# Random-feature attention with two gated layers on one core: the feature projections of units 4 to 15 as pairs of half-height float32 products

## The chip, the cores and the metric

The kernel runs on one core of one Trainium2 chip. The metric is the device time of one execution in microseconds (us), as the median of three executions. Everything below is read from one profiled execution of the kernel before the change. The engines are TensorE (PE, with its weight loads listed apart as PEld), VectorE (DVE), ScalarE (ACT), GpSimd (POOL), and SyncE (SP), which only issues transfers here.

## The reference

Three stages follow one another. The first is attention with random features for 4 batches of 8 heads, 576 rows of 64 numbers and 128 features; the other two are a gated layer over 2304 tokens and a softly routed layer of 8 experts.

```python
def phi(x):
    proj = np.einsum('bhsd,md->bhsm', x, omega)
    sq = np.sum(x * x, axis=-1, keepdims=True) / 2.0
    h = proj - sq
    h = h - np.max(h, axis=-1, keepdims=True)
    return np.exp(h) / np.sqrt(m)
q_p, k_p = (phi(q_s), phi(k_s))
kv = np.einsum('bhsm,bhsd->bhmd', k_p, v)
z = np.sum(k_p, axis=2)
num = np.einsum('bhsm,bhmd->bhsd', q_p, kv)
den = np.einsum('bhsm,bhm->bhs', q_p, z)[..., None] + 1e-06
...
x = _moe_ref(x=x, **moe_kwargs)      # sigmoid(x @ w_gate) * (x @ w_val) @ w_out
return _moe2_ref(x=x, **moe2_kwargs) # soft routing into 8 experts of 4 slots
```

The change touches only `proj`, and how the features `h` are kept and turned.

## The kernel before, in words

A **unit** is one batch and two heads; there are 16, four for each batch. The two heads of a unit share the 128 partitions of a tile: head 0 has its 64 numbers on partitions 0 to 63, head 1 on 64 to 127. The 576 rows of K and of Q come as four whole tiles of 128 rows each; the last 64 rows of K and the last 64 of Q share one more tile, the tail. So a unit has nine tiles to project.

For each unit these pieces of code run:

- `load_unit` and `prep_qk` fetch the rows and compute their squared norms into `SQ`. From unit 10 on (`N_PROJ`), `prep_qk` also splits K and Q into a high and a low part (`hi_of` with the engines of `SITE["hqk"]`, `lo_of` with `SITE["lqk"]`), in a second format (fp32r).
- `chunk_proj(u, i)` makes the features in five chunks: K tiles 0 and 1, K tiles 2 and 3, the tail, Q tiles 0 and 1, Q tiles 2 and 3. A tile is one product of TensorE: the tile stands still in the array, and `obf`, 128 rows by 256 columns, streams past it. `obf` holds the feature matrix twice, for head 0 in rows 0 to 63 and columns 0 to 127, for head 1 in the other rows and columns, with zeros elsewhere. Units 0 to 9 do this in float32; units 10 to 15 use `three`, which is three products of the split parts. Each chunk fills one bank of PSUM. VectorE then takes each 128 by 128 piece out of it, adds the norm and finds the row's extreme (`tensor_tensor_reduce`), and ScalarE takes the exponential of each piece.
- `chunk_kv` multiplies the K features with V: 10 products of 128 columns, in float32.
- `chunk_qT` turns the Q features with TensorE. For the tail it turns only the lower 64 partitions of the tile: two transposes of 64 partitions.
- `chunk_num` makes numerator and denominator, half the rows at a time. For units 0 to 9 these are float32 products of 288 columns that write to 64 partitions each.

K features, Q features and tail features have one buffer each (`HK`, `HQ`, `HT`), so the features of unit u+1 can be written only when unit u has read its own.

The gated layer (`gate`, `val`, `down`) is by far the most work: per step 36 fp32r products, mostly of 512 columns, into the PSUM banks `ga`, `va` and `o0` to `o3`. It runs through `GROUPS` of token blocks. Block j needs the attention of batch j.

The order of the work is not the order of the code. `Plan.schedule` records all instructions, gives each a cost (`Plan.cost`) and a key (its due time less a lead), and lists them engine by engine. Each engine then works strictly in the order that it was given. The attention and the routed layer share two PSUM banks named `fl` (`NFL` = 2); at the start they may also use `o0` to `o3`. A tile of `fl` that is used for the first time needs a free bank, and in the plan it is parked until there is one. Some element-wise work may go to either of two engines, as `SITE` lists them.

Of the kernel before, what the change touches and what calls it, by code (L numbers as in the profile page):

```python
# [45 lines left out]
SITE = {  # L46
    "hqk": ("DVE", "ACT"), "lqk": ("POOL", "DVE"), "hqt": ("ACT", "DVE"),
    "hx": ("ACT", "DVE"), "lx": ("POOL", "DVE"), "hg": ("DVE", "ACT"),
# [7 lines left out]
T0 = -60  # L56
N_PROJ = 10
N_NUM = 10
# [26 lines left out]
SIZE = {F32: 4, F32R: 4, I32: 4, U32: 4, I64: 8}  # L85
HOP = 0.16


# [10 lines left out]
class Plan:  # L99


    def __init__(self, nc):
        self.eng = {"PE": nc.tensor, "ACT": nc.scalar, "DVE": nc.vector, "POOL": nc.gpsimd, "SP": nc.sync}
        self.ops = []
        self.tiles = {}
        self.tags = {}
        self.t = 0.0
        self.lead = {}
        self.floor = 0.0
        self.floors = []  # L110
        self.hist = {}


# [22 lines left out]
    def add(self, alts):  # L136
# [4 lines left out]
        if "out" not in kw and rest:  # L141
            outs.append(rest.pop(0))
        ins += rest
        i = len(self.ops)
        pe = alts[0][0] == "PE"
# [33 lines left out]
    def cost(self, eng, method, kw, outs, ins):  # L179


        o = outs[0] if outs else None
# [30 lines left out]
    def schedule(self):  # L213
# [12 lines left out]
        nv = n  # L226
        dyn_of = [None] * n
        left = {}
        for tag, info in self.tags.items():
            gens = info["gens"]  # L230
            if info["dyn"]:
                for g, acc in enumerate(gens):
                    left[tag, g] = len(acc)
                    for a in acc:
                        dyn_of[a] = (tag, g)
                continue
# [85 lines left out]
        while ev:  # L322
            now = ev[0][0]
            while ev and ev[0][0] <= now + 1e-9:
                _, kind, x = heapq.heappop(ev)
                if kind == 1:
                    offer(x)
                elif kind == 2:
                    d = dyn_of[x]
                    left[d] -= 1  # L330
                    if left[d] == 0:
                        room[d[0]] += 1
                        for p in parked[d[0]]:
                            offer(p)
                        parked[d[0]] = []
            for e in E:
                while free_at[e] <= now + 1e-9:
# [4 lines left out]
                    backlog[p[0]] -= self.cost(p[0], p[1], p[3], ops[i][4], ops[i][5])[0]  # L342
                    d = dyn_of[i]
                    if d and d not in live:
                        if room[d[0]] == 0:
                            if i not in parked[d[0]]:
                                parked[d[0]].append(i)
                            continue
                        room[d[0]] -= 1
                        live.add(d)  # L350
                    alts, _, _, _, outs, ins, lazy = ops[i]
# [18 lines left out]
                    heapq.heappush(ev, (free_at[e], 0, -1))  # L370
                    if d:
                        heapq.heappush(ev, (end + HOP, 2, i))
# [4 lines left out]
    def issue(self):  # L377
        for _, _, (e, method, a, k) in self.schedule():
            getattr(self.eng[e], method)(*a, **k)  # L379


def body(ctx, tc, nc, qkT, tok, von, omT, wall, phi, w1, w2, ident_d, srep_d, rrep_d, mask_d, out):
# [70 lines left out]

    q0, q1 = region(0, F32), half_region(0, F32)
# [3 lines left out]
    QT = KV = XK = XQ = obh = obl = None  # L458

    def split_regions():  # L460

        nonlocal QT, KV, XK, XQ, obh, obl
        g0, g1 = region(0, F32R), half_region(1, F32R)
        QT = carve(g0, 0, [2, 2, S])
        KV = carve(g0, 2304, [2, 2, 128])
        XK = carve(g0, 2816, [2, 640])
        XQ = carve(g1, 0, [2, 512])
        obh = carve(g1, 1024, [256])
        obl = carve(g1, 1280, [256])
        hi_of(obh, obf, ("DVE",))  # L470
        lo_of(obl, obf, obh, ("DVE",))

# [4 lines left out]
    obf = carve(g3, 3712, [256])  # L477
    HK = carve(g4, 0, [4, 2, M])
    HQ = carve(g4, 1024, [4, 2, M])
    HT = carve(g4, 2048, [1, 2, M])  # L480
    RR = [carve(g4, 2304 + 288 * k, [HALF]) for k in range(2)]
# [3 lines left out]
    SQ = carve(g4, 3712, [18])  # L485
    MX = [carve(g4, 3730 + 8 * k, [2, 4]) for k in range(6)]
    ring = {}
# [21 lines left out]
    def prep_qk(u, kind):  # L509

        if u >= NU:
            return
        if u == N_PROJ and kind == 0:
            split_regions()
        x, c, t, n = ((XK, slice(0, 640), 0, 5), (XQ, slice(640, 1152), 5, 4))[kind]
        src = QKTs[u % 2][:, c]
# [10 lines left out]
    def prep_first(a, e):  # L527
# [4 lines left out]
        DVE.tensor_reduce(out=SQ[:, 2 * a:2 * e], in_=w, axis=AX.X, op=ALU.add)  # L532

    def chunk_proj(u, i):
# [6 lines left out]
        psv = ps.rearrange("p (t m) -> p t m", t=2)  # L541
        for t in range(nt):
            c = slice(c0 + 128 * t, c0 + 128 * t + 128)
# [4 lines left out]
        n = 2 * nt  # L548
        sq = SQ[:, g0:g0 + n]
        flat = ps.rearrange("p (g m) -> p g m", m=M)[:, 0:n, :]  # L550
        hv = hb.rearrange("p t h m -> p (t h) m")
        low = turn(MX, "mx")[:, 0, 0:n]
        for g in range(n):
            DVE.tensor_tensor_reduce(out=hv[:, g], in0=flat[:, g], in1=sq[:, g:g + 1].to_broadcast([128, M]),
                                     scale=1.0 / 16.0, scalar=BIG, op0=ALU.add, op1=ALU.min, accum_out=low[:, g:g + 1])
        for g in range(n):
            ACT.activation(out=hv[:, g], in_=hv[:, g], func=AF.Exp, scale=-1.0, bias=low[:, g:g + 1])

    def chunk_kv(u):

        ps = bank()[:, 0:256].rearrange("p (h c) -> p h c", h=2)
        for h in range(2):
            for t in range(NT):
                k = HK[:, t, h, :] if t < 4 else HT[:, 0, h, :]
                PE.matmul(ps[:, h, :], k, Vs[u % 2][:, t, h, :], start=t == 0, stop=t == NT - 1)
# [7 lines left out]
    def chunk_qT(u, i):  # L573
        ps = bank().rearrange("p (h n) -> p h n", h=2)
        n = (256, 256, 64)[i]
        for h in range(2):
            if i == 2:
                PE.transpose(ps[:, h, 0:64], HT[64:128, 0, h, :], ident[64:128, 64:128])
                continue
            for t in range(2):  # L580
                PE.transpose(ps[:, h, 128 * t:128 * t + 128], HQ[:, 2 * i + t, h, :], ident)
        if u < N_NUM:
            copy(QTF[:, :, 256 * i:256 * i + n], ps[:, :, 0:n], SITE["hqt"])
            return
        qh, ql = (QT[:, l, :, 256 * i:256 * i + n] for l in range(2))
        hi_of(qh, ps[:, :, 0:n], SITE["hqt"])
        lo_of(ql, ps[:, :, 0:n], qh, ("DVE",))

# [37 lines left out]
    def step_chunks(u):  # L626
# [11 lines left out]
        def last():  # L638
            chunk_proj(v, 4)
            prep_qk(u + 2, 0)  # L640

        c = [kv, P(0), lambda: chunk_qT(u, 0), P(1), lambda: chunk_qT(u, 1), lambda: chunk_qT(u, 2), P(2),
             lambda: chunk_num(u, 0), P(3), lambda: chunk_num(u, 1), last]
        own = (0, 2, 4, 5, 7, 9)
        if v >= NU:
# [442 lines left out]
    prep_first(0, 2)  # L1088
    chunk_proj(0, 0)
    prep_first(2, 5)  # L1090
    prep_qk(0, 1)
    chunk_proj(0, 1)
    chunk_proj(0, 2)
    SP.dma_start(out=TOK, in_=tok[1])
    SP.dma_start(out=Vs[1], in_=von[1])
    chunk_proj(0, 3)
    chunk_proj(0, 4)
    prep_qk(1, 0)
# [185 lines left out]
```

## Time and profile before

| | |
|---|---|
| median of 3 runs | 703.87 us (703.55 to 704.65) |
| span of the profiled execution, first to last instruction | 702.4 us |
| TensorE busy | 678.3 us, 97% |
| VectorE, ScalarE busy | 445.7 and 443.1 us, 63% each |
| GpSimd busy | 301.3 us, 43% |

The page gives no other time for the profiled execution than its span. The span is 1.5 us (0.2%) under the median of the runs; the times of rows below are added up against the span, and the difference is then taken from the median. Rows of a timeline give the start, the length from the first start to the last end, the engine, and the operation with its count. A float32 product stands in the trace as two rows (the order of the program has 2 where the trace has 4), an fp32r product or a transpose as one.

### The profile page before, as it was taken

What the parts mean: (1) busy time and instruction counts of PE and PEld (TensorE: products, weight loads), DVE (VectorE), ACT (ScalarE), POOL (GpSimd) and SP (SyncE); (2) the same over time, 40 slices, a digit from 0 to 9 for tenths busy, and PEclk for the clock granted to TensorE, in tenths of its full rate; (3) what the DMA queues carried; (4) which work ended last, traced back from release to release, by engine and by line L of the source; (5) the groups of instructions that cost most, each with busy time, mean ns of one, the idle gap of its engine ahead of it and who ended that gap; (6) DMA issues with size and microseconds to landing.
All of it is one profiled execution on the core that took longest, in us unless ns stands there. A gap on an engine that the chain in (4) does not pass through costs nothing.

```text
span 702.4 us, 12029 instructions
## 1 busy us (share of the span) xinstructions
PE 678.3 (97%) x4095; PEld 543.9 (77%) x4095; DVE 445.7 (63%) x1292; ACT 443.1 (63%) x987; POOL 301.3 (43%) x255
## 2 busy tenths in 40 slices
PE   8999999999989999999999999999999999999993
PEld 6677667777767788788888888778888788998662
DVE  4898997899997554657476765555454335766221
ACT  5999898888777565856567674654444444765021
POOL 0356545546454444644444444354444444642000
PEclk9999999999999999999999999999999999999998
DMA  7878777677866335443333334469422228557897
GB/s 279 297 253 308 249 229 255 227 257 271 267 238 201 123 114 206 148 133 108 133 135 132 90 115 142 127 231 330 166 91 90 91 83 281 168 162 250 320 407 235
DMA packets 50124, 139.47 MB, mean 199 GB/s; under 512 B 5520, under 2 KB 11152, under 8 KB 50064
## 3 DMA queue, kind: packets, MB, share of 16 engines
q1 hardware_dynamic: 45456, 121.94, 51.9%
q10 hardware_dynamic: 4608, 16.78, 6.9%
q8 instruction: 32, 0.52, 0.3%
q14 instruction: 28, 0.23, 0.1%
HBM read 124.54 MB, written 14.16 MB: 197 GB/s over the span
## 4 chain that ended last, share of the span: by engine, by line
PE 67%; DVE 4%; issue 3%; ACT 2%; DMA 2%; POOL 1%; POOLq 0%; ACTq 0%; DVEq 0%
PE o L379 19%; PE ga L379 18%; PE va L379 18%; PE fl L379 12%; DVE x2T L379 2%; DMA ws<-wscr 1%; DVE g L379 1%; DVE ga_a L379 1%; ACT ga_a L379 1%; DMA g<-in_wall 1%; POOL w L379 1%; ACT g L379 0%; ACT XT L379 0%; ACT gt L379 0%; ACT x2T L379 0%
## 5 line engine op out<-in xcount | busy, mean ns | idle before, releaser
L379 POOL TENSOR_TENSOR w<-ws,w 128x512 fp32r<-128x512 f32 x141 | 188.3, 1336 | 235.7 <-ACT w L379 132.5
L379 PE MATMUL ga<-XT,w 128*128 128x512 f32 (+1 forms) x720 | 169.4, 377 | 1.8 <-DVE ga_a L379 1.0
L379 PE MATMUL va<-XT,w 128*128 128x512 f32 (+1 forms) x720 | 167.6, 376 | 1.2 <-DVE ga_a L379 1.2
L379 PE MATMUL o<-gt,w 128*128 128x512 f32 (+1 forms) x720 | 165.3, 374 | 0.9 <-ACT w L379 0.8
L379 PEld LDWEIGHTS ga<-XT,w 128*128 128x128 f32 x720 | 123.8, 189 | 28.1 <-issue 3.0
L379 PEld LDWEIGHTS va<-XT,w 128*128 128x128 f32 x720 | 123.5, 189 | 27.1 <-issue 3.7
L379 PEld LDWEIGHTS o<-gt,w 128*128 128x128 f32 x720 | 123.6, 189 | 25.1 <-issue 2.6
L379 ACT ACTIVATE g<-g 128x128 f32<-128x128 f32 (+3 forms) x340 | 121.1, 415 | 18.9 <-DVE g L379 12.9
L379 ACT ACTIVATE w<-ws 128x512 fp32r<-128x512 f32 x107 | 67.3, 629 | 61.9 <-issue 19.8
L379 PE MATMUL fl<-g,g 128*128 128x128 f32 (+2 forms) x514 | 87.8, 343 | 3.2 <-DVE g L379 2.1
L379 PEld LDWEIGHTS fl<-g,g 128*128 128x128 f32 (+1 forms) x514 | 61.8, 179 | 22.5 <-issue 6.6
L379 ACT ACTIVATE ga_a<-ga_a 128x512 f32<-128x512 f32 (+1 forms) x120 | 70.2, 585 | 12.6 <-DVE ga_a L379 11.5
L379 ACT ACTIVATE ga_a<-ga 128x512 f32<-128x512 f32 (+1 forms) x60 | 33.2, 554 | 65.4 <-PE ga L379 65.3
L379 DVE CUSTOM_DVE_ANT_0 g<-fl,g 128x128 f32<-128x128 f32 x242 | 56.9, 286 | 19.5 <-PE fl L379 19.0
L379 DVE SCALAR_TENSOR_TENSOR ga_a<-ga,ga_a 128x512 f32<-128x512 f32 (+1 forms) x60 | 38.2, 636 | 46.4 <-ACT ga_a L379 46.1
L379 DVE CAST w<-ws 128x512 fp32r<-128x512 f32 x55 | 23.8, 432 | 67.8 <-PE ga L379 38.1
L379 ACT ACTIVATE x2T<-g 128x512 f32<-128x512 f32 x72 | 45.9, 670 | 5.8 <-DVE x L379 5.7
L379 DVE TENSOR_SCALAR x2T<-x2T 128x512 f32<-128x512 f32 (+1 forms) x72 | 47.7, 670 | 0.9 <-ACT x2T L379 0.8
L379 DVE TENSOR_TENSOR ga_a<-va,ga_a 128x512 f32<-128x512 f32 (+1 forms) x60 | 38.0, 634 | 15.3 <-ACT ga_a L379 11.9
L379 POOL TENSOR_TENSOR XT<-g,XT 128x288 fp32r<-128x288 f32 (+2 forms) x46 | 31.3, 690 | 32.0 <-ACT XT L379 29.5
L379 ACT ACTIVATE ga_a<-ga_a,one_b 128x512 f32<-128x512 f32 (+1 forms) x60 | 40.8, 679 | 1.2
L379 DVE TENSOR_TENSOR g<-fl,g 64x288 f32<-64x288 f32 (+3 forms) x57 | 27.6, 485 | 15.5 <-ACT g L379 12.5
(200 smaller groups left out, 752.6 us busy)
## 6 DMA issues: line engine op xcount, KB each, us to landing
ws<-wscr SPq DMA_DIRECT2D x42, 512.0 KB, 3.6
ws<-wscr SPq DMA_DIRECT2D x78, 256.0 KB, 2.8
g<-in_wall SPq DMA_DIRECT2D x36, 512.0 KB, 4.9
g<-in_von SPq DMA_DIRECT2D x16, 640.0 KB, 5.1
wscr<-x SPq DMA_DIRECT2D x36, 256.0 KB, 4.5
g<-in_qkT SPq DMA_DIRECT2D x15, 576.0 KB, 4.8
g<-in_tok SPq DMA_DIRECT2D x15, 576.0 KB, 5.0
g<-in_w ACTq DMA_DIRECT2D x16, 512.0 KB, 5.2
```

Source lines behind the costliest of these rows:

```text
L379: getattr(self.eng[e], method)(*a, **k)
```

## The change

Units 4 to 15 project a group of four tiles (K, and again Q) in one go. Each tile is now two products, one for each head: head h uses only the 64 partitions of its half, for the tile as well as for the feature matrix, so that 128 columns stream instead of 256. The products of head 0 write to one bank, those of head 1 to a second. The eight products are recorded as one item (`together`) that the plan places in one piece, with its two banks. The tail remains one product of 256 columns. Units 0 to 3 keep their five chunks (`ROWS` = 4). All units now project in float32, so the split of K and Q from unit 10 on is gone, with its buffers. In place of them there are two buffers each for K, Q and tail features, by turns of units. `chunk_qT` turns the whole tail tile (128 partitions) and copies the half that it needs. In `Plan.cost` three numbers change, and `schedule` can handle an item with two banks.

```diff
 def chunk_proj(u, i):
-        x, c0, nt, hb, g0 = ((XK, 0, 2, HK[:, 0:2], 0), (XK, 256, 2, HK[:, 2:4], 4), (XK, 512, 1, HT, 8),
-                             (XQ, 0, 2, HQ[:, 0:2], 10), (XQ, 256, 2, HQ[:, 2:4], 14))[i]
-        ps = bank()
...
-            if u < N_PROJ:
-                PE.matmul(psv[:, t], QKTs[u % 2][:, 640 * (i > 2) + c0 + 128 * t:][:, 0:128], obf, start=True, stop=True)
-            else:
-                three(psv[:, t], (x[:, 0, c], x[:, 1, c]), (obh, obl))
...
+        c0, nt, hb, t0, g0 = PARTS[i]
+        hb = hb[u % 2][:, t0:t0 + nt]
+        x = QKTs[u % 2][:, c0:c0 + 128 * nt]
...
+            ps = [bank()[:, 0:128 * nt].rearrange("p (t m) -> p t m", m=M) for _ in range(2)]
...
+                if nt < 4:
+                    PE.matmul(both[:, t].rearrange("p h m -> p (h m)"), x[:, 128 * t:128 * t + 128], obf,
+                              start=True, stop=True)
+                    continue
+                for h in range(2):
+                    r = slice(64 * h, 64 * h + 64)
+                    PE.matmul(ps[h][:, t], x[r, 128 * t:128 * t + 128], obf[r, 128 * h:128 * h + 128],
+                              start=True, stop=True)
+        plan.together(products, [SQ[:, g0:g0 + 2 * nt]], [hb])
...
+        for h in range(2):
+            for t in range(nt):
+                g = 2 * t + h
+                DVE.tensor_tensor_reduce(out=hb[:, t, h], in0=ps[h][:, t],
 def prep_qk(u, kind):
-        if u >= N_PROJ:
-            hi_of(x[:, 0, :], src, SITE["hqk"])
-            lo_of(x[:, 1, :], src, x[:, 0, :], SITE["lqk"])
 def chunk_qT(u, i):
-                PE.transpose(ps[:, h, 0:64], HT[64:128, 0, h, :], ident[64:128, 64:128])
+                PE.transpose(ps[:, h, 0:128], HTs[u % 2][:, 0, h, :], ident)
 def step_chunks(u):
+        if v < ROWS:
+            c = [kv, P("K0"), qT[0], P("K1"), qT[1], qT[2], P("T"), num[0], P("Q0"), num[1], last]
+        else:
+            c = [kv, P("K"), qT[0], qT[1], qT[2], P("T"), num[0], num[1], last]
 def cost(self, eng, method, kw, outs, ins):
-                return max(n / 600.0, 0.21) / 2 + 0.02, False
-            return (0.416 if ins[0].ap[0][1] == 64 else max(0.222, n / 600.0)), False
+                return max(n / 600.0, 0.21) / 2 + 0.12, False
+            return (max(0.222, n / 600.0) / 2 if ins[0].ap[0][1] == 64 else max(0.222, n / 600.0)), False
...
-                return 0.16 + ni / 960.0, False
+                return 0.075 + ni / 960.0, False
```

How this moves the work on TensorE is seen in two places of its order. In the rows, `ga`, `va` and `o0` to `o3` are products of the gated layer; `fl` are the two shared banks, with the number of the tile. `g2` holds K and Q, `g3` the feature matrix and V, `g4` and `g1b` the features.

The first place is unit 6, in the first group of the gated layer. Before, TensorE has there the product of K features and V (10 products), the two K chunks of unit 7, the transposes of Q between them, and the tail's transposes of 64 columns:

```order
L379 MATMUL fl_197<-g3_78,g4_79 128x128 x10
L379 MATMUL fl_198<-g3_78,g2_77 128x256 x2
L379 MATMUL fl_202<-ident_63,g4_79 128x128 x4
L379 MATMUL ga_216<-XT_96,w0_201 128x512 x5
L379 MATMUL fl_203<-g3_78,g2_77 128x256 x2
L379 MATMUL fl_207<-ident_63,g4_79 128x128 x4
L379 MATMUL va_222<-XT_96,w1_206 128x512 x4
L379 MATMUL fl_208<-ident_63,g4_79 128x64 x2
```

Of the change, at the same place:

```order
L402 MATMUL fl_198<-g3_79,g4_80 128x128 x10
L402 MATMUL va_206<-XT_97,w1_190 128x512 x10
...
L402 MATMUL fl_202<-g3_79,g2_78 128x128
L402 MATMUL fl_203<-g3_79,g2_78 128x128
L402 MATMUL fl_202<-g3_79,g2_78 128x128
L402 MATMUL fl_203<-g3_79,g2_78 128x128
...
L402 MATMUL ga_216<-XT_97,w0_201 128x512 x6
L402 MATMUL fl_204<-ident_63,g4_80 128x128 x4
L402 MATMUL ga_216<-XT_97,w0_201 128x512 x2
L402 MATMUL fl_205<-ident_63,g4_80 128x128 x4
L402 MATMUL ga_216<-XT_97,w0_201 128x512
L402 MATMUL fl_209<-ident_63,g4_80 128x128 x2
```

Where two chunks of two products of 256 columns stood apart, eight products of 128 columns now stand in one piece (four of them are shown) and go by turns to two banks. The tail's transposes are 128 columns wide.

The second place is the step from unit 10 to unit 11, where the projection was in three fp32r products for each tile. Before:

```order
L379 MATMUL fl<-g_78,g_79 128x128 x10
L379 MATMUL o_257<-gt,w_343 128x512 x3
...
L379 MATMUL fl<-g1b,g_311 128x256 x6
L379 MATMUL ga<-XT,w_348 128x512 x12
L379 MATMUL fl<-ident,g_79 128x128 x4
L379 MATMUL va<-XT,w_352 128x512 x12
L379 MATMUL fl<-g1b,g_311 128x256 x6
```

Of the change:

```order
L402 MATMUL fl<-g_79,g_80 128x128 x10
L402 MATMUL o_258<-gt,w_342 128x512 x3
...
L402 MATMUL fl<-g_79,g_78 128x128 x8
L402 MATMUL ga<-XT,w_347 128x512 x12
L402 MATMUL fl<-ident,g_80 128x128 x4
L402 MATMUL va<-XT,w_352 128x512 x12
L402 MATMUL fl<-ident,g_80 128x128 x4
```

Twelve products of 256 columns in two chunks have become eight products of 128 columns in one, and the gated layer's products around them stay whole.

## Rows read from the trace of the kernel before

**Rows 1.** The page: busy times, and 40 slices (tenths).

```profile
PE 678.3 (97%) x4095; PEld 543.9 (77%) x4095; DVE 445.7 (63%) x1292; ACT 443.1 (63%) x987; POOL 301.3 (43%) x255
...
PEclk9999999999999999999999999999999999999998
```

**Rows 2.** Windows: start, end, length, busy time (count) of PE, PEld, DVE, ACT, POOL, clock.

```profile
0.00:31.00 31.00, 27.81 (x141) 20.30 (x141) 17.89 (x95) 21.70 (x60) 6.00 (x11) 1.00 0.83 294
31.00:143.00 112.00, 110.48 (x585) 81.05 (x584) 98.77 (x359) 101.42 (x262) 59.10 (x54) 1.00 0.76 253
143.00:275.00 132.00, 127.89 (x627) 101.35 (x626) 101.61 (x242) 95.56 (x200) 62.96 (x50) 1.00 0.62 206
275.00:345.00 70.00, 69.40 (x401) 57.52 (x400) 42.52 (x129) 46.43 (x99) 36.57 (x32) 1.00 0.42 140
345.00:478.00 133.00, 132.43 (x725) 110.38 (x725) 80.91 (x240) 82.54 (x178) 58.31 (x50) 1.00 0.44 145
```

**Rows 3.** Waits of PE: who waited for whom, us, times, longest.

```profile
PE fl L379 <- DVE g L379: 5.2, 9, 1.8
```

**Rows 4.** Timeline of PE: the gated layer's products alone, then 10 float32 products of 128 columns.

```profile
152.93 0.62 PE L379 MATMUL o<-gt,w 128*128 128x512 f32 x2
153.38 0.61 PE L379 MATMUL ga<-XT,w 128*128 128x512 f32 x2
153.84 0.62 PE L379 MATMUL va<-XT,w 128*128 128x512 f32 x2
154.29 1.98 PE L379 MATMUL o<-gt,w 128*128 128x512 f32 x8
156.10 2.39 PE L379 MATMUL fl<-g,g 128*128 128x128 f32 x20
158.25 0.94 PE L379 MATMUL ga<-XT,w 128*128 128x512 f32 x3
```

**Rows 5.** Timeline of PE around a float32 chunk of two tiles (unit 8).

```profile
149.19 1.20 PE L379 MATMUL va<-XT,w 128*128 128x512 f32 x4
150.22 1.02 PE L379 MATMUL fl<-g,g 128*128 128x256 f32 x4
150.89 1.28 PE L379 MATMUL va<-XT,w 128*128 128x512 f32 x4
```

**Rows 6.** Timeline of PE around an fp32r chunk of two tiles (unit 10).

```profile
230.97 0.85 PE L379 MATMUL o<-gt,w 128*128 128x512 f32 x3
231.66 0.88 PE L379 MATMUL fl<-g1b,g 128*128 128x256 f32 x6
232.37 1.09 PE L379 MATMUL ga<-XT,w 128*128 128x512 f32 x4
```

**Rows 7.** Timeline of PE around one and around two pairs of 64-column-half products.

```profile
103.22 1.29 PE L379 MATMUL o<-gt,w 128*128 128x512 f32 x5
104.45 0.71 PE L379 MATMUL fl<-g,g 128*64 128x288 f32 x4
105.08 0.96 PE L379 MATMUL o<-gt,w 128*128 128x512 f32 x3
...
243.70 1.07 PE L379 MATMUL ga<-XT,w 128*128 128x512 f32 x4
244.70 1.19 PE L379 MATMUL fl<-g,g 128*64 128x288 f32 x8
245.82 1.43 PE L379 MATMUL va<-XT,w 128*128 128x512 f32 x5
```

**Rows 8.** Timeline of PE around the tail's transposes, and around four whole transposes.

```profile
92.39 0.85 PE L379 MATMUL o<-gt,w 128*128 128x512 f32 x3
93.17 0.34 PE L379 MATMUL fl<-ident,g 64*128 64x64 f32 x2
93.44 0.73 PE L379 MATMUL o<-gt,w 128*128 128x512 f32 x2
...
193.97 1.31 PE L379 MATMUL o<-gt,w 128*128 128x512 f32 x5
195.12 0.60 PE L379 MATMUL fl<-ident,g 128*128 128x128 f32 x4
195.47 0.93 PE L379 MATMUL ga<-XT,w 128*128 128x512 f32 x3
```

**Rows 9.** Groups of PE between 31 and 143 us: count, busy us, mean ns, idle before.

```profile
L379 PE MATMUL fl<-g,g 128*128 128x256 f32 x90 | 23.8, 386 | 0.7 <-DVE g L379 0.7
...
L379 PE MATMUL o<-g,g 128*128 128x256 f32 x18 | 4.8, 391 | 0.0
...
L379 PE MATMUL fl<-ident,g 64*128 64x64 f32 x10 | 1.7, 247 | 0.0
...
L379 PE MATMUL o<-ident,g 64*128 64x64 f32 x2 | 0.3, 248 | 0.0
```

**Rows 10.** Groups over the whole span: the splits of K in units 10 to 15.

```profile
L379 POOL TENSOR_TENSOR g<-g,g 128x640 fp32r<-128x640 f32 x5 | 8.0, 1606 | 2.9 <-ACT g L379 2.4 <-issue 0.5
...
L379 DVE CAST g<-g 128x640 fp32r<-128x640 f32 x4 | 3.0, 747 | 1.1 <-PE fl L379 1.1
```

**Rows 11.** Timeline of DVE in a chunk of unit 5: the extremes of four pieces.

```profile
67.81 0.28 DVE L379 CUSTOM_DVE_ANT_0 g<-fl,g 128x128 f32<-128x128 f32 x1
...
68.43 0.09 DVE L379 DVE_READ_ACCUMULATOR2_ANT g<- 128x1 f32 x1
```

More of the change, by code (lines that the diff above doesn't have):

```diff
@@ L56 @@
 T0 = -60
-N_PROJ = 10
+N_SPLIT = 10
 N_NUM = 10
@@ L86 @@
 HOP = 0.16
+TURN = 0.2
+ROWS = 4
 class Eng:
@@ L111, in __init__, with together @@
         self.hist = {}
+        self.bundle = None
+    def together(self, calls, first=(), then=()):
+        self.bundle = []
+        calls()
+        parts, self.bundle = self.bundle, None
+        self.place([(parts[0][0][0], "together", (), {"parts": parts})],
+                   [o for _, outs, _ in parts for o in outs] + list(then),
+                   [i for _, _, ins in parts for i in ins] + list(first))
     def tile(self, pool, shape, dtype, tag, bufs=1, dyn=False):
@@ L143, in add, with place @@
         ins += rest
+        if self.bundle is not None:
+            self.bundle.append((alts[0], outs, ins))
+        else:
+            self.place(alts, outs, ins)
+    def place(self, alts, outs, ins):
         i = len(self.ops)
@@ L179, in cost @@
     def cost(self, eng, method, kw, outs, ins):
+        if method == "together":
+            return TURN * (len(kw["parts"]) > 2) + sum(self.cost(eng, a[1], a[3], o, i)[0] for a, o, i in kw["parts"]), False
         o = outs[0] if outs else None
@@ L226, in schedule @@
         nv = n
-        dyn_of = [None] * n
+        dyn_of = [[] for _ in range(n)]
         left = {}
@@ L328, in schedule @@
                 elif kind == 2:
[L329 to L335, printed above, removed]
+                    for d in dyn_of[x]:
+                        left[d] -= 1
+                        if left[d] == 0:
+                            room[d[0]] += 1
+                            for p in parked[d[0]]:
+                                offer(p)
+                            parked[d[0]] = []
             for e in E:
@@ L342, in schedule @@
                     backlog[p[0]] -= self.cost(p[0], p[1], p[3], ops[i][4], ops[i][5])[0]
[L343 to L347, printed above, removed]
+                    fresh = [d for d in dyn_of[i] if d not in live]
+                    if fresh:
+                        tag = fresh[0][0]
+                        first = any(ops[q][1] < ops[i][1] for q in parked[tag])
+                        if room[tag] < len(fresh) or first:
+                            if i not in parked[tag]:
+                                parked[tag].append(i)
                             continue
-                        room[d[0]] -= 1
-                        live.add(d)
+                        room[tag] -= len(fresh)
+                        live.update(fresh)
                     alts, _, _, _, outs, ins, lazy = ops[i]
@@ L378, in issue @@
         for _, _, (e, method, a, k) in self.schedule():
-            getattr(self.eng[e], method)(*a, **k)
+            for e, method, a, k in [p[0] for p in k["parts"]] if method == "together" else [(e, method, a, k)]:
+                getattr(self.eng[e], method)(*a, **k)
 def body(ctx, tc, nc, qkT, tok, von, omT, wall, phi, w1, w2, ident_d, srep_d, rrep_d, mask_d, out):
@@ L477, in body @@
     obf = carve(g3, 3712, [256])
-    HK = carve(g4, 0, [4, 2, M])
-    HQ = carve(g4, 1024, [4, 2, M])
-    HT = carve(g4, 2048, [1, 2, M])
+    HKs = [carve(r, 0, [4, 2, M]) for r in (g4, q2)]
+    HQs = [carve(r, 1024, [4, 2, M]) for r in (g4, q2)]
+    HTs = [carve(g4, at, [1, 2, M]) for at in (2048, 3792)]
     RR = [carve(g4, 2304 + 288 * k, [HALF]) for k in range(2)]
@@ L485, in body @@
     SQ = carve(g4, 3712, [18])
-    MX = [carve(g4, 3730 + 8 * k, [2, 4]) for k in range(6)]
+    MX = [carve(g4, 3730 + 8 * k, [8]) for k in range(6)]
     ring = {}
@@ L548, in chunk_proj @@
[L548 to L557, printed above, removed]
+        c0, nt, hb, t0, g0 = PARTS[i]
@@ new lines, in chunk_proj, with products @@
+        hb = hb[u % 2][:, t0:t0 + nt]
+        x = QKTs[u % 2][:, c0:c0 + 128 * nt]
+        if nt < 4:
+            both = bank()[:, 0:256 * nt].rearrange("p (t h m) -> p t h m", h=2, m=M)
+            ps = [both[:, :, h] for h in range(2)]
+        else:
+            ps = [bank()[:, 0:128 * nt].rearrange("p (t m) -> p t m", m=M) for _ in range(2)]
+        def products():
+            for t in range(nt):
+                if nt < 4:
+                    PE.matmul(both[:, t].rearrange("p h m -> p (h m)"), x[:, 128 * t:128 * t + 128], obf,
[5 more added lines that the diff above has]
+                              start=True, stop=True)
@@ new lines, in chunk_proj @@
+        plan.together(products, [SQ[:, g0:g0 + 2 * nt]], [hb])
+        low = turn(MX, "mx")
+        for h in range(2):
+            for t in range(nt):
+                g = 2 * t + h
+                DVE.tensor_tensor_reduce(out=hb[:, t, h], in0=ps[h][:, t],
+                                         in1=SQ[:, g0 + g:g0 + g + 1].to_broadcast([128, M]),
+                                         scale=1.0 / 16.0, scalar=BIG, op0=ALU.add, op1=ALU.min,
+                                         accum_out=low[:, g:g + 1])
@@ L559, in chunk_kv @@
+        for h in range(2):
+            for t in range(nt):
+                g = 2 * t + h
+                ACT.activation(out=hb[:, t, h], in_=hb[:, t, h], func=AF.Exp, scale=-1.0, bias=low[:, g:g + 1])
     def chunk_kv(u):
@@ L563, in chunk_kv @@
             for t in range(NT):
-                k = HK[:, t, h, :] if t < 4 else HT[:, 0, h, :]
+                k = HKs[u % 2][:, t, h, :] if t < 4 else HTs[u % 2][:, 0, h, :]
                 PE.matmul(ps[:, h, :], k, Vs[u % 2][:, t, h, :], start=t == 0, stop=t == NT - 1)
@@ L638, in last @@
         def last():
-            chunk_proj(v, 4)
+            chunk_proj(v, "Q1" if v < ROWS else "Q")
             prep_qk(u + 2, 0)
-        c = [kv, P(0), lambda: chunk_qT(u, 0), P(1), lambda: chunk_qT(u, 1), lambda: chunk_qT(u, 2), P(2),
-             lambda: chunk_num(u, 0), P(3), lambda: chunk_num(u, 1), last]
-        own = (0, 2, 4, 5, 7, 9)
+        qT = [lambda i=i: chunk_qT(u, i) for i in range(3)]
+        num = [lambda i=i: chunk_num(u, i) for i in range(2)]
+        if v < ROWS:
+            c = [kv, P("K0"), qT[0], P("K1"), qT[1], qT[2], P("T"), num[0], P("Q0"), num[1], last]
+            own = (0, 2, 4, 5, 7, 9)
+        else:
+            c = [kv, P("K"), qT[0], qT[1], qT[2], P("T"), num[0], num[1], last]
+            own = (0, 2, 3, 4, 6, 7)
         if v >= NU:
```

50 lines of the change are left out of this document (21 added, 29 removed).

## The prediction, made before the changed kernel ran

> **What bounds the kernel now.** I read the page first. TensorE is busy for 97% of the span, no other engine for more than 63%, and its granted clock is full in all slices but the last [rows 1]. So time taken from TensorE's own work is time saved, where TensorE does not wait for somebody else. The windows tell where that is [rows 2]. From 275 to 478 us TensorE is busy for 99.4% and VectorE and ScalarE for 61 and 64%: whatever TensorE is spared there comes off the span. From 31 to 143 us TensorE is busy for 110.5 of 112.0 us, but ScalarE for 101.4 and VectorE for 98.8; both together have 200.2 of 224 us filled. TensorE leads there by little. Before 31 us it is idle for 3.2 us, and the units that run there keep most of their old form. Of its own waits, the one for VectorE to empty an `fl` bank is the largest, and it is 5.2 us in 9 times [rows 3].
>
> A busy time of TensorE does not tell what a group costs, since products overlap in it. I use ends instead. The gated layer's products of 512 columns follow one another at (154.29 - 152.93)/6 = 0.227 us [rows 4]. Where a group stands between two rows of such products, its cost is the end of the row behind less the end of the row ahead, less 0.227 us for each product of the row behind. So:
>
> - float32 chunk of two tiles: (150.89 + 1.28) - (149.19 + 1.20) - 4 x 0.227 = 0.87 us, or 0.436 a tile [rows 5].
> - fp32r chunk of two tiles: 233.46 - 231.82 - 0.91 = 0.73 us, or 0.366 a tile [rows 6].
> - 10 float32 products of 128 columns: 159.19 - 156.27 - 0.68 = 2.24 us, and each is two rows, so 0.112 us a row [rows 4].
> - one pair of float32 products that use half the array's columns: 106.04 - 104.51 - 0.68 = 0.85 us; two such pairs together: 247.25 - 244.77 - 1.135 = 1.345 us [rows 7]. The second pair adds 0.50 us, so 0.35 us of each group is not for its products: it goes with the change from the whole array to halves and back.
> - the tail's two transposes of 64 partitions: 94.17 - 93.24 - 0.45 = 0.48 us. Four whole ones: 196.40 - 195.28 - 0.68 = 0.44 us, or 0.110 each [rows 8].
>
> **The change part by part.** *Four tiles in row halves.* Eight products make 16 rows of 128 columns. One after another they take 16 x 0.112 = 1.79 us. If the halves work side by side it is 0.90 us. To either comes the turn of the array into halves and back. No row shows two row halves at work, so this has to be bounded. For side by side speaks the pair in column halves: its four rows of 288 columns would take 4 x 0.112 x 288/128 = 1.01 us one after another, and 0.50 us was added [rows 7]; overlap there is whole. The turn is 0.35 us by those rows; for the one operation that uses half the rows, the tail's transposes, it is 0.48 - 2 x 0.110 = 0.26 us if a half transpose costs as much as a whole one, and more if it costs less [rows 8]. I take 0.90 + 0.35 = 1.25 us for four tiles, with 1.16 us as the lower and 1.79 + 0.35 = 2.14 us as the upper bound. Before, four tiles cost 1.74 us (float32) or 1.46 us (fp32r). That saves 0.49 us in each of 12 groups of units 4 to 9, 5.9 us, and 0.21 us in each of 12 groups of units 10 to 15, 2.6 us.
>
> The Trainium skill says the same of the turn (TensorEngine Tiling (Array Packing), Key Properties): changing the tiling mode drains TensorE. It gives no time; the 0.35 us of [rows 7] stands for it, and 24 groups pay it, 8.4 us that the saving above has already lost.
>
> *Tail tile in float32* for units 10 to 15: 0.436 instead of 0.366 us, six times, 0.4 us lost. *Whole tail transposed:* 0.22 instead of 0.48 us, 0.26 us saved a unit. The copy out still takes 64 columns. I count units 2 to 15, since the first two are turned before about 31 us: 3.6 us.
>
> *Splits removed.* A K split is 1.6 us on GpSimd and 0.75 us on VectorE or ScalarE [rows 10], the Q split a little less. GpSimd is busy for less than half of the time then [rows 2]; I take nothing for it, but some 1.4 us a unit come free on VectorE and ScalarE.
>
> *Two feature buffers* let a unit's features be written while the last unit's are still read. At most this gives back a part of the 5.2 us of [rows 3]; I take nothing.
>
> *Two banks at once.* The eight products take both `fl` banks. VectorE empties a piece in 0.21 us [rows 11], so the first bank is free about 0.85 us after the group and the second 1.7 us after it. Until then no other product of the attention can start. The order puts products of the gated layer behind each group, six of them in the first place shown, which is 1.4 us of cover. Where VectorE is late, TensorE stands still at the next `fl` product, and the gated layer, which is queued behind it, with it. I take nothing, and price it below.
>
> *New cost numbers* give a new order everywhere. Nothing in the profile tells its sign; I allow 1 us either way.
>
> **The sum by stage.** Full, it is 5.9 + 2.6 - 0.4 + 3.6 = 11.7 us. Between 31 and 143 us stand 108 rows of float32 projections, six units, and 12 of half transposes, six tails [rows 9]. Five of these units change: 5 x 0.99 + 6 x 0.26 = 6.5 us. If that came off whole, VectorE and ScalarE would have to fill 200.2 of 211 us, 95%, against 89% now. I take 4.0 us (93%). From 143 to 275 us there are unit 9, units 10 and 11, and three tails: 0.99 + 2 x 0.36 + 0.77 = 2.5 us; TensorE is idle for 4.1 us there already [rows 2], and I take 2.1. Behind it four units and five tails give 2.7 us, and I take 2.6. Together 8.7 us: the span goes from 702.4 to 693.7 us, and the median, 1.5 us above it, to 695.2 us.
>
> **The rivals.** *The halves go one after another.* Each of the 16 rows loads weights of 128 columns, where four tiles before had 8 such loads in float32. A row of 128 columns and its load take 0.112 us together [rows 4], and if the two halves must take turns at loading, this is the price of every row. The column halves of [rows 7] do not rule it out, since each loads only 64 columns and streams 288. Then four tiles cost 2.14 us, 12 x 0.40 + 12 x 0.68 = 12.9 us more than before; with the tails it is 12.9 + 0.4 - 3.6 = 9.7 us slower, 713.6 us. It decides from 1.74 us for four tiles on: there the loss in the fp32r units eats the tails' gain. Chance 0.13.
>
> The Trainium skill has a rule for each side of this. TensorE: Matmul & The Clock Gate (LDWEIGHTS (loading the stationary operand)) says that a load takes its columns over 1.2 GHz whatever its rows, 107 ns for 128; the 0.112 us of [rows 4] agrees, and with loads in turn it would give the 713.6 us. TensorEngine Tiling (Array Packing), Key Properties, says that different tiles can load and multiply in parallel, which would give the 695.2 us; no row of the trace bears on it.
>
> *The two banks become the wait.* If each of the 24 groups makes TensorE stand still for 0.36 us, the 8.7 us are gone, 703.9 us. For it: VectorE is 88% busy in the first stage. Against it: TensorE seldom waits for these banks now, and the gated layer always has products ready. Chance 0.08.
>
> *ScalarE and VectorE take over the first stage.* Then it gives 1 us of its 6.5, and the median is 698.2 us, up to 702 with some waits for banks. Chance 0.14.
>
> *All of it comes through*, since work that is not urgent moves out of the first stage: 11.7 us, 692.2 us, with the cheaper turn 690.5. Chance 0.08.
>
> **The numbers.** My forecast keeps 0.57: 695.2 us, between 692.5 and 697.5. The range of 690.5 to 702.5 us takes in the forecast, the full gain and the first stage held back, and leaves out the halves in turn and most of the bank wait, 0.2. About 0.2% (1.4 us) can be told from no change. Faster is 0.57 + 0.14 + 0.08 = 0.79, same 0.08, slower 0.13.
>
> **What would show it.** Right: in a timeline, eight products of 64 partitions and 128 columns between two rows of the gated layer cost about 1.25 us by the same reckoning, and their rows start in pairs; the tail's transposes cost 0.22 us; from 275 us on the same number of gated products ends 2.6 us sooner relative to the stage's start. If the groups cost 2.1 us, the halves go in turn. If they cost 1.25 us and the span is the same, the waits of TensorE for VectorE at `fl` have grown, or its idle time between 31 and 143 us has. The prediction fails if the turn into row halves costs far more than 0.35 us, or if the new order makes waits at places that the change doesn't touch.

## The result, and the profile after

The changed kernel takes 696.56 us (median of 4 runs, 695.52 to 697.65), the kernel before in the same series 703.71 us (703.08 to 704.65). The ratio is 0.9898, with a 95% interval of 0.9869 to 0.9927: 1.0% faster. 695.2 us were forecast. The span of the profiled execution went from 702.4 to 695.8 us.

The page of the changed kernel answers to [rows 1]. TensorE's busy time fell by 9.7 us, and its idle time rose by 3 us:

```profile
PE 668.6 (96%) x4233; PEld 533.3 (77%) x4233; DVE 452.3 (65%) x1305; ACT 428.7 (62%) x962; POOL 285.6 (41%) x241
```

A timeline of TensorE around a group of four tiles in row halves, and around a tail's transposes (start, length, operation, count), answers to [rows 5, 6 and 8]:

```profile
65.71 2.10 PE L402 MATMUL ga<-XT,w 128*128 128x512 f32 x8 [0.66 <-DVE ga_a L402]
67.74 1.16 PE L402 MATMUL fl<-g,g 64*128 64x128 f32 x16
68.83 1.20 PE L402 MATMUL ga<-XT,w 128*128 128x512 f32 x4
...
233.07 1.53 PE L402 MATMUL va<-XT,w 128*128 128x512 f32 x6
234.44 0.38 PE L402 MATMUL fl<-ident,g 128*128 128x128 f32 x2
234.57 1.64 PE L402 MATMUL o<-gt,w 128*128 128x512 f32 x6
```

By the prediction's reckoning this group costs (68.83 + 1.20) - (65.71 + 2.10) - 4 x 0.227 = 1.31 us; 21 of the 24 groups cost 1.25 to 1.31 us, the other three 1.58 to 1.95 us. Two whole transposes cost 236.21 - 234.60 - 6 x 0.227 = 0.25 us. Sixteen rows of 0.112 us each have a length of only 1.16 us, and in the trace they start two by two, 7 ns apart: the halves work side by side.

The windows of the changed kernel answer to [rows 2]:

```profile
31.00:143.00 112.00, 107.68 (x669) 78.52 (x670) 106.44 (x371) 97.97 (x252) 61.11 (x55) 1.00 0.77 263
143.00:275.00 132.00, 129.80 (x683) 101.90 (x682) 103.67 (x246) 92.23 (x197) 59.07 (x49) 1.00 0.63 206
275.00:345.00 70.00, 69.05 (x418) 55.43 (x416) 44.24 (x129) 44.91 (x98) 25.30 (x22) 1.00 0.42 135
345.00:478.00 133.00, 132.75 (x741) 109.48 (x741) 78.78 (x240) 80.21 (x177) 56.84 (x49) 1.00 0.47 154
```

The reader is to see two different things. From 345 us on TensorE has as little idle time as before. Between 31 and 143 us it now waits for 4.3 us (before, 1.5), and VectorE is busy for 106.4 us instead of 98.8. One such wait, of 1.7 us, stands in the timelines of TensorE and of VectorE:

```profile
84.23 0.39 PE L402 MATMUL ga<-XT,w 128*128 128x512 f32 x1
86.34 1.16 PE L402 MATMUL fl<-g,g1b 128*128 128x128 f32 x8 [1.71 <-DVE g L402]
```

```profile
82.25 3.19 DVE L402 TENSOR_SCALAR x2T<-x2T 128x512 f32<-128x512 f32 x3
85.36 0.28 DVE L402 CUSTOM_DVE_ANT_0 g1b<-fl,g 128x128 f32<-128x128 f32 x1
```

VectorE was held up by three operations that took 3.19 us, and began late to empty the two banks of a group, and TensorE stood at its next product into an `fl` bank.

Where the time went can be read from the starts of the gated layer's groups, that is, from the first `ga` product of a group in each run's timeline. The table has them in us for the kernels below, each from its profiled execution; that of e8 was a slow one (836.7 us), so e8 is not in the table. Up to the third group, and behind it, the work is the same in all of them, apart from what the edits change. At the start of the second group it is not: the plan moves pieces of the attention across that point.

| kernel | second group starts | third starts | from third to fifth | fifth to end |
|---|---|---|---|---|
| before | 143.3 | 275.1 | 202.8 | 224.4 |
| changed | 144.4 | 271.1 | 201.5 | 223.2 |
| e1_tail_only | 141.8 | 273.6 | 201.4 | 222.8 |
| e2_rows_from_8 | 146.1 | 271.1 | 201.5 | 221.9 |
| e3_head_by_head | 145.9 | 275.2 | 205.7 | 225.3 |
| e4_old_costs | 144.4 | 280.3 | 200.5 | 223.1 |
| e5_one_buffer | 151.2 | 278.7 | 201.5 | 221.5 |
| e6_turn_as_measured | 143.4 | 277.8 | 201.0 | 221.4 |
| e7_new_costs_alone | 148.8 | 278.2 | 202.8 | 222.0 |
| e9_old_reduction_cost | 143.9 | 280.5 | 200.5 | 221.8 |
| e10_rows_8_q_on_scalar | 146.5 | 274.4 | 200.3 | 224.2 |
| e11_turn_03 | 143.9 | 274.2 | 201.9 | 222.5 |
| e12_turn_01 | 137.3 | 267.4 | 201.0 | 224.5 |

The change gained 4.0 us before the third group, 1.3 us from the third to the fifth, and 1.2 us behind that. The last 1.2 us stand where both kernels do the same work; that stretch takes 221.4 to 225.3 us in the kernels of the table.

One execution need not lie at its kernel's median: that of e3 took 2.0 us more, that of e5 2.8 us less. And TensorE's clock has a share in the table. In the changed kernel's execution the granted clock fell from 2.4 to 1.2 GHz for 3.4 us, at 14.5 us, behind a wait for a transfer. In the experiment e3 below, which has the same work there, it did not. The first row of each pair has the same ten products in both; the second is a window as in [rows 2], where the third number from the end is the clock as a share of 2.4 GHz. The changed kernel:

```profile
13.26 3.46 PE L402 MATMUL o<-g,g 128*128 128x128 f32 x20 [3.04 <-DMA g<-in_von]
...
14.50:17.90 3.40, 3.40 (x18) 3.40 (x18) 0.00 (x0) 0.98 (x4) 0.98 (x1) 0.50 1.02 406
```

e3:

```profile
13.11 2.47 PE L402 MATMUL o<-g,g 128*128 128x128 f32 x20 [2.95 <-DMA g<-in_von]
...
14.50:17.90 3.40, 2.88 (x26) 2.41 (x26) 0.30 (x1) 1.64 (x4) 1.25 (x1) 1.00 1.01 413
```

At 18.9 us the changed kernel is 1.75 us behind e3 in the same work, and VectorE is still as far behind at 55 us. Of the profiled executions, those of before, e1, e2, e3, e10 and e12 had no such fall ahead of the third group. Those of the changed kernel, e6 (14.4 us) and e11 (176.7 us) had one of 3.4 us, those of e5 (22.5 us) and e7 (166.9 us) one of 6.8 us, and those of e4 and e9 two each.

### The profile page after: what moved, and what is told of

Read it like the earlier page. It is cut to its first block, busy times and chain, and to the rows that moved or that the text cites. A ratio compares the mean times of both kernels' runs of the same rounds, so it can differ in the third digit from the quotient of the medians.

```text
span 695.8 us, 12239 instructions
## 1 busy us (share of the span) xinstructions
PE 668.6 (96%) x4233; PEld 533.3 (77%) x4233; DVE 452.3 (65%) x1305; ACT 428.7 (62%) x962; POOL 285.6 (41%) x241
## 4 chain that ended last, share of the span: by engine, by line
PE 80%; DVE 9%; DMA 4%; issue 2%; ACT 1%; SPq 1%; POOL 0%; POOLq 0%; ACTq 0%; DVEq 0%
PE o L402 24%; PE ga L402 20%; PE va L402 20%; PE fl L402 15%; DVE x2T L402 3%; DVE g L402 2%; DMA wscr<-x 2%; DVE x L402 1%; DMA g<-in_von 1%; DMA g<-in_tok 1%; DVE g1b L402 1%; DVE ga_a L402 1%; SPq L402 1%; DMA g<-in_wall 1%; DVE gt L402 1%
## 5 line engine op out<-in xcount | busy, mean ns | idle before, releaser
L402 POOL TENSOR_TENSOR w<-ws,w 128x512 fp32r<-128x512 f32 x135 | 177.6, 1316 | 245.8 <-ACT w L402 134.1
L402 PE MATMUL o<-gt,w 128*128 128x512 f32 (+1 forms) x720 | 167.3, 376 | 0.9 <-ACT w L402 0.8
L402 ACT ACTIVATE w<-ws 128x512 fp32r<-128x512 f32 x107 | 67.2, 628 | 62.5 <-PE o L402 18.9
L402 PE MATMUL fl<-g,g 64*128 64x128 f32 (+3 forms) x702 | 82.9, 314 | 4.4 <-DVE g L402 2.1
L402 ACT ACTIVATE g<-g 128x128 f32<-128x128 f32 (+3 forms) x204 | 73.1, 412 | 13.5 <-DVE g L402 8.3
L402 PEld LDWEIGHTS fl<-g,g 64*128 64x128 f32 (+2 forms) x702 | 58.9, 179 | 27.3 <-DVE g L402 7.6
L402 DVE TENSOR_SCALAR x2T<-x2T 128x512 f32<-128x512 f32 (+1 forms) x72 | 45.3, 645 | 1.8 <-ACT x2T L402 1.8
L402 POOL TENSOR_TENSOR XT<-g,XT 128x288 fp32r<-128x288 f32 (+2 forms) x44 | 33.8, 781 | 25.0 <-ACT XT L402 23.6
L402 ACT ACTIVATE g1b<-g1b,g 128x128 f32<-128x128 f32 x128 | 40.0, 388 | 6.1 <-DVE g L402 6.1
L402 DVE TENSOR_TENSOR gt<-ga_a,gt 128x512 fp32r<-128x512 f32 (+1 forms) x54 | 38.1, 706 | 2.2 <-ACT gt L402 1.3
```

## The experiments

Each ratio is to the kernel before, run on the same chip in the same series, with its 95% interval. The changed kernel has 0.9898.

**e1_tail_only.** The kernel before, with whole tails transposed and the half that is needed copied:

```diff
-                PE.transpose(ps[:, h, 0:64], HT[64:128, 0, h, :], ident[64:128, 64:128])
+                PE.transpose(ps[:, h, 0:128], HT[:, 0, h, :], ident)
...
```

> The kernel before with one part of the change: the whole tail tile is transposed (128 columns) and half of it copied. Theory (TensorE's own time sets the span, except in the first stage, where VectorE now sets it): the tail's transposes cost 0.23 us instead of 0.48, 0.25 us in each of 8 to 14 units, so 2.0 to 3.5 us off: 700.2 to 701.7 us. Rival (the gain of the whole change comes from the new order, the new cost numbers and the two buffers, not from shorter work on TensorE): 703 to 704.5 us, no change.

Measured: 700.38 us, ratio 0.9958 (0.9943 to 0.9973), some 3 us off. The theory holds. About two fifths of the gain come with this one edit.

**e2_rows_from_8.** The changed kernel, with

```diff
-ROWS = 4
+ROWS = 8
```

> The changed kernel with row halves only from unit 8 on (ROWS = 8); units 4 to 7 project in their five chunks as before. Theory (the first stage, to about 144 us, is set by VectorE, so shorter products on TensorE there are worth nothing): within 0.8 us of the changed kernel's 696.6 us. Rival (what TensorE saves there counts in full): 4 units x 0.9 us = 3.6 us more, 700.2 us.

Measured: 696.41 us, ratio 0.9904 (0.9881 to 0.9928), the same as the changed kernel. In the table the third group starts at 271.1 us in both. Row halves in units 4 to 7, 3.6 us of TensorE's time, are worth little in this order: nothing by the table, and up to 1.75 us if the fall of the clock in the changed kernel's execution is taken off. Why that is so, this run does not tell.

**e3_head_by_head.** The changed kernel, with all products of head 0 in a group before those of head 1:

```diff
-            for t in range(nt):
+            for h, t in [(h, t) for h in range(2) for t in range(nt)]:
...
```

> The changed kernel, but within a group of four tiles all products of head 0 come first and then all of head 1, so that neighbours in the order use the same row half. Theory (the gain of a group is that the two halves work side by side): a group takes 16 x 0.112 + 0.40 = 2.2 us instead of 1.30, in 24 groups 21 us, of which some 16 to 21 show: 713 to 718 us. Rival (a product of 64 partitions is cheaper by itself, or TensorE starts products of the second half ahead of the first): 696 to 699 us.

Measured: 706.04 us, ratio 1.0043 (1.0025 to 1.0061): the gain is gone, though less is lost than the theory said. The timeline of TensorE at the group that was shown above:

```profile
64.75 2.11 PE L402 MATMUL ga<-XT,w 128*128 128x512 f32 x8 [0.75 <-DVE ga_a L402]
66.78 1.71 PE L402 MATMUL fl<-g,g 64*128 64x128 f32 x16
68.42 1.20 PE L402 MATMUL ga<-XT,w 128*128 128x512 f32 x4
```

The group costs 69.62 - 66.86 - 0.91 = 1.85 us: neither 1.31 nor the 2.19 us (16 x 0.112 + 0.40) of no overlap. Its 16 rows are 1.71 us long, 0.55 us more than in turns. In the traces VectorE, ScalarE and GpSimd do the same operations in the same order as in the changed kernel, so this run also tells what a microsecond more of TensorE costs. Ahead of the third group stand 15 groups. They became longer by 7.8 us in all: 0.54 us each, but for one in which the changed kernel itself waited. The third group starts 4.1 us later, and e3 had been 1.75 us ahead in the same work before the first of these groups, since its clock had not fallen; so it lost 5.9 us, three quarters. From the third to the fifth, nine groups became longer by 4.3 us in all, and the stretch by 4.2 us: nearly all of it.

**e4_old_costs** and **e9_old_reduction_cost.** The changed kernel, with the plan's two other prices as before, and with one of them as before:

```diff
-                return max(n / 600.0, 0.21) / 2 + 0.12, False
+                return max(n / 600.0, 0.21) / 2 + 0.02, False
...
-                return 0.075 + ni / 960.0, False
+                return 0.16 + ni / 960.0, False
```

e9 has only the second of the two.

> The changed kernel with two of the plan's cost numbers as before: 0.02 instead of 0.12 us added for a product in column halves, 0.16 instead of 0.075 us for VectorE's reduction. All work stays, only the order moves. Theory (shorter work on TensorE makes the gain): 695.5 to 698.5 us. Rival (the new numbers make the order that gains): 700 to 704 us.

> The changed kernel with VectorE's reduction priced at 0.16 us more than its columns, as before, instead of 0.075; the column halves keep the new price. Theory (it is this number that made the order with old costs lose, since 18 reductions a unit are planned 0.085 us too long): 703 to 706 us. Rival (it is the column price, or both together): 696 to 699 us.

Measured: 705.02 us, ratio 1.0022 (1.0004 to 1.0040), and 704.93 us, ratio 1.0031 (1.0016 to 1.0046). e4 lies 1 us above its rival's range, e9 within its theory's. The whole gain is gone with the price of VectorE's reduction, although most groups cost the same 1.30 us there. The table puts the loss between the second and the third group. The waits of TensorE between 143 and 275 us in e4 (who waited for whom, us, times, longest):

```profile
PE ga L402 <- DVE ga_a L402: 5.7, 4, 2.2
```

In the changed kernel TensorE's largest wait there is one for `fl`, 2.1 us in 3 times. A timeline of e4 shows how one of the four came about:

```profile
160.45 1.28 POOL L402 TENSOR_TENSOR w<-ws,w 128x512 fp32r<-128x512 f32 x1 [1.02 <-ACT w L402]
160.55 1.73 DVE L402 SCALAR_TENSOR_TENSOR x2T<-g,x2T 128x512 int32<-128x512 int32 x1
...
162.20 0.68 DVE L402 SCALAR_TENSOR_TENSOR ga_a<-ga,ga_a 128x512 f32<-128x512 f32 x1
...
162.93 0.74 PE L402 MATMUL ga<-XT,w 128*128 128x512 f32 x2 [1.22 <-DVE ga_a L402]
```

An operation of VectorE that needs 0.68 us at other times took 1.73 us beside one of GpSimd. The gate's operation behind it came late, and TensorE waited 1.2 us for the bank `ga`. Waits are not all of the loss. In e4 the clock was at 1.2 GHz for 3.4 us at 32.1 us and again at 192.5 us, in e9 for 3.4 us at 55.1 us and for 6.8 us at 215.5 us; each time TensorE had just waited for 2.0 to 3.5 us. Here are the wait and the fall of e9 between the second and the third group:

```profile
216.12 1.23 PE L402 MATMUL fl<-g,g 128*64 128x288 f32 x4 [3.48 <-DVE g L402]
...
215.50:222.40 6.90, 6.28 (x16) 4.35 (x17) 3.42 (x8) 4.06 (x8) 1.32 (x2) 0.51 0.34 114
```

Over a whole execution the granted clock was 0.984 to 0.991 in e9's runs and 0.991 to 0.996 in the changed kernel's. The middles lie 0.006 apart; as an estimate, 0.006 x 700 us is 4 us of TensorE's work, half of what e9 loses.

**e5_one_buffer.** The changed kernel, with one buffer of each kind:

```diff
-    HKs = [carve(r, 0, [4, 2, M]) for r in (g4, q2)]
+    HKs = [carve(r, 0, [4, 2, M]) for r in (g4, g4)]
```

and likewise for Q and tail.

> The changed kernel with one buffer for each kind of features instead of two. Theory (shorter work on TensorE makes the gain, and the buffers matter little, since the order keeps the features of the next unit behind the readers of the last): 696 to 699 us. Rival (without the second buffer the groups of four, which write twice as many features in one piece, wait for their readers): 700 to 704 us.

Measured: 706.28 us, ratio 1.0046 (1.0026 to 1.0066). Slower than either range. The loss stands before the second group, which starts at 151.2 us. The order is another there from the start (the gated layer's first product comes at 22.7 us instead of 28.8), and the clock fell there for 6.8 us, so the run does not separate waits for readers from the change of order.

**e7_new_costs_alone.** The kernel before, with the two new prices of e4.

> The kernel before with the two new cost numbers alone (0.12 for column halves, 0.075 for VectorE's reduction). Theory (numbers and shorter work belong together: the numbers only let the shorter work show): 701.5 to 704 us. Rival (the better order is the gain, 8 us, as their removal from the changed kernel suggests): 694 to 698 us.

Measured: 704.82 us, ratio 1.0023 (1.0000 to 1.0047). This is 0.8 us above the theory's range and far from the rival's: the new numbers alone gain nothing. Two more parts of the plan changed that no run has alone: the price of products of 64 partitions, and a rule that nothing may take a free bank while something due earlier waits for one.

**e6_turn_as_measured, e11_turn_03, e12_turn_01.** The changed kernel with another price of the turn of the array in the plan; the work is the same:

```diff
-TURN = 0.2
+TURN = 0.4
```

> The changed kernel with the plan's price for the turn of the array at 0.4 us, as the trace has it, instead of 0.2. No work changes, only the order. Theory (the order as such is robust; only an error in VectorE's price hurts): 695.5 to 698 us. Rival (any other order loses some us by chance, as the old cost numbers did): 699 us or more.

> The changed kernel with the plan's price of the turn at 0.3 us: the same work in one more order. Theory that the order decides 5 us either way before 275 us: the span from 275 us on stays within 0.7 us of the changed kernel's 424.7 us, and the start of the third group of the gated layer lies anywhere between 270 and 281 us. Rival (0.4 us was a single bad order): 696 to 698 us.

> The changed kernel with the plan's price of the turn at 0.1 us: another order of the same work. The two theories expect the same as for 0.3 us.

Measured: with 0.4, 701.95 us, ratio 1.0002 (0.9980 to 1.0024); with 0.3, 700.63 us, ratio 0.9972 (0.9951 to 0.9992); with 0.1, 693.81 us, ratio 0.9867 (0.9853 to 0.9882). My theory for 0.4, that the order is robust, fell. Of the ranges for 0.3 and 0.1 the first came true; with 0.1 the third group starts sooner than the 270 to 281 us that I gave. The third group starts at 277.8, 274.2 and 267.4 us; from the third to the fifth group all three are within 0.5 us of the changed kernel's 201.5 us, and their spans from the third group on are 422.5 to 425.5 us against 424.7. So the rest of the kernel keeps its gain, and what is gained before 275 us hangs on the order. With 0.1 the kernel is 0.3% faster than the changed one by the two ratios (four runs of 693.1 to 694.7 us); their intervals still overlap. The four prices stand in order of their times, 693.8, 696.6, 700.6 and 702.0 us, though the turn's own price is 0.4 in the trace. Four points do not tell whether that is a rule.

**e8_turned_q_on_scalar** and **e10_rows_8_q_on_scalar.** The changed kernel, and e2, with the turned Q copied by ScalarE alone:

```diff
-    "hqt": ("ACT", "DVE"),
+    "hqt": ("ACT",),
```

> The changed kernel, but the turned Q is copied by ScalarE alone (before, VectorE may take it too, and does so for some 10 copies of 0.68 us in the first stage). Theory (VectorE sets the first stage, ScalarE has 14 us to spare there): 2 to 4 us less than the changed kernel, 692.5 to 695 us. Rival (which order the plan happens to make decides some 5 us either way in the first two stages, whatever is reasoned about it): anywhere from 697 to 704 us.

> The same with row halves only from unit 8 on. Theory: as e8, 692.5 to 695.5 us, since row halves before unit 8 are worth nothing. Rival: 697 to 704 us.

Measured: 702.29 us, ratio 0.9987 (0.9971 to 1.0002), and 700.71 us, ratio 0.9967 (0.9953 to 0.9980). Both are slower than without the edit. The windows of e2 and of e10 from 31 to 143 us:

```profile
31.00:143.00 112.00, 110.71 (x607) 82.03 (x603) 102.95 (x374) 102.88 (x262) 59.36 (x55) 1.00 0.75 266
```

```profile
31.00:143.00 112.00, 108.58 (x595) 81.05 (x594) 97.01 (x359) 101.97 (x264) 56.99 (x52) 1.00 0.75 255
```

VectorE was relieved by 5.9 us there, and the second group started no sooner (146.5 us instead of 146.1). So the busy time of VectorE alone does not set that stage in this order, and the theory with which I had explained e2 fell. Whether VectorE and ScalarE together set it, these runs do not tell; ScalarE stayed at 102 of 112 us. e12 does not speak against VectorE either. The windows from the first group's start to the second's, of the changed kernel and of e12:

```profile
28.83:144.44 115.61, 111.15 (x687) 79.96 (x684) 109.85 (x374) 101.56 (x259) 64.60 (x58) 1.00 0.76 260
```

```profile
27.03:137.34 110.31, 107.58 (x672) 78.87 (x671) 102.84 (x360) 99.07 (x253) 65.28 (x58) 1.00 0.76 263
```

In e12 VectorE has 7.0 us less to do up to there, and the second group starts 7.1 us sooner.

## Why the prediction was right, point by point

**The halves work side by side.** Right. A group was priced at 1.25 us and costs 1.30 or 1.31 us; its products take the 0.90 us of half the rows, and the turn takes 0.40 us instead of the 0.35 us that the column halves show [rows 7]. Over 24 groups that is 1.4 us, and three dearer groups add 1.2 us. The rival of halves in turn would have shown 2.14 us and 713.6 us. The Trainium skill's rule that different tiles load and multiply in parallel (TensorEngine Tiling (Array Packing), Key Properties) is what this trace shows: two rows of 0.112 us pass in 0.112 us, each with its own load of weights. e3 shows what the kernel would be without most of that.

**The tail.** Right: 0.25 us instead of 0.48, where 0.22 us were forecast, and by e1 some 3 us of the whole gain.

**Two banks at once.** The forecast put nothing for it and priced the rival at 0.36 us a group. TensorE's waits for VectorE at `fl` hardly grew in the whole kernel, from 5.2 us in 9 times [rows 3] to 6.1 us in 10. The rival did not come true, though the 1.7 us at 86 us is a case of it.

**The sum by stage.** This step failed, though its total came out: 8.7 us were forecast, the span fell by 6.6 us. Before the third group I took 6.1 us and 4.0 came. Behind it I took 2.6 and 2.6 came, but that is luck: 1.2 us of it stand behind the fifth group, where no projection is left, and 1.3 us where the change is. How the 4.0 us divide between the first two stages cannot be said, since the plan moved work from the second into the first: at the start of the second group VectorE and ScalarE together have done 5 us more than before. The rival that the first stage gives almost nothing may still be true; by e2, at most half of what units 4 to 7 spared TensorE came through. Its reason, that VectorE and ScalarE are full, is not shown: e10 speaks against VectorE alone, and no run relieves both. What is shown is e3: with the order held, a microsecond more of TensorE costs three quarters of one before 275 us and nearly all of it behind. TensorE was spared some 8 us before 275 us (0.43 us in each of 12 groups, 0.25 us in nine tails, and little for units 10 and 11). Three quarters of that are 6 us. The 4.0 us that were seen and the 1.75 us that went to the clock come near it, but the order moved as well, so that this is an estimate and no proof.

**The new cost numbers.** This is the term that was mis-sized. I allowed 1 us either way. The order that they make is worth 8 us (e4, e9), and a change of a single price moves the time between 693.8 and 702.0 us with the same work. The orders that were tried start the third group anywhere from 267.4 to 280.5 us, and the kernel before with new prices and old work (e7) falls in the same spread. The forecast's range was wide enough for the order that the change happened to bring, not for all of these: that the time came out as forecast is in part luck. Nor did the forecast have a term for the clock, and bad orders pay through it as well: in e4 and e9 it fell behind long waits.

**Two feature buffers.** I took nothing. Without them the kernel is 10 us slower (e5), but the order is another too, and how much of it belongs to the buffers stays open.

**What stays open.** Which operation's lateness sets the stages before 275 us is known for single waits only (the one at 86 us, the ones in e4 and e9), not in general. Nor is it known why lower prices of the turn make better orders.

## What to carry to other kernels

Price a new form of an operation by the ends of steady rows around it, and bound what is new by the nearest forms: the turn into column halves told the cost of the turn into row halves to 0.05 us, where busy times would have told nothing.

Before a microsecond of the leading engine is counted as a microsecond of the kernel, ask stage by stage what it is worth; lengthening the same work in the same order, as e3 did, measures just that. Look at the granted clock of both executions first: here one fall of 3.4 us, left out of account, would have made half of three quarters.

Where a planner makes the order from prices, an edit of a price is an edit of the whole kernel. Run a few neighbouring prices before a gain or a loss of 1% is put down to the work itself.

## What the runs showed of the hardware that was not expected

The turn of TensorE into row halves and back costs 0.40 us (1.30 us, as most groups cost, less 8 pairs of 0.112 us), a little more than the 0.35 us for column halves.

In e3 the products of the second half did not wait for those of the first. Sixteen rows in order, of which only the last of head 0 and the first of head 1 could overlap, would take 15 x 0.112 + 0.40 = 2.08 us; the group took 1.85 us. In the trace three pairs of its rows start within 0.01 us of each other, at 67.33, 67.55 and 67.66 us, where that order allows one pair. A reading that fits is that TensorE begins products of the free half ahead of several that stand before them in the order; no other run tests it.

An element-wise operation on VectorE of 512 columns took 1.73 us instead of 0.68 beside a subtraction on GpSimd (e4). The changed kernel has 36 operations of this kind: the 20 beside which GpSimd hardly works take 0.67 to 0.69 us, the 12 beside which it works for at least half of their time 0.67 to 1.74 us, 1.22 us in the middle. Three of another kind in a row took 3.19 us in the changed kernel (at 82 us), with GpSimd at work beside them, where single ones take 0.42 us at other times.

The granted clock of TensorE fell to 1.2 GHz for 3.4 or 6.8 us ahead of the third group in seven of the thirteen executions of the table. Each fall began inside a wait of TensorE of 2.0 to 3.9 us, or at most 1.4 us behind it. Such a wait did not always bring one: e3 waited 2.95 us at 10 us and e10 2.78 us at 189 us, and the clock stayed at 2.4 GHz.
